# Re-planning a fused attention and mixture-of-experts kernel: a new table of planner constants, and five pieces of work moved or cut finer

## The chip, the cores and the metric

The kernel runs on one core of a Trainium2 chip. The metric is device time in microseconds, the median of several runs. Five engines work side by side, each through its own queue in order: PE (matrix products), ACT (activations), DVE (vector operations), POOL (vector operations and indirect transfers), and SP, which here only issues transfers.

## What is computed

Windowed causal attention over 8 sequences of 576 tokens with 8 heads of 64, then a mixture of 8 experts on its 4608 rows of 512, each row going to its two best experts:

```python
scores = scale * q @ k.T + slope[h] * -|i - j|      # only 0 <= i - j < 128
x = (softmax(scores) @ v) as (4608, 512)
noisy = x @ w_gate + log1p(exp(x @ w_noise)) * noise
top2, weights = two largest of noisy, softmax over the two
out[row] = sum over its two experts e of weight * (relu(x[row] @ w1[e]) @ w2[e])   # 512 -> 1024 -> 512
```

## The kernel before

**A planner writes the program.** The kernel function describes the work as strands (Python generators). Each strand yields operations with an engine, an expected duration and a rank. `Order` (L111) runs them against its own clock: whenever an engine is free it takes the waiting operation of lowest rank (`take`, L171) and writes it into that engine's queue. So the order in all five queues is fixed when the kernel is built, by expected durations and by ranks, which come from the table at L43 to L72. `either` (L280) offers an operation to ACT and, at a rank later by an entry of `LATE`, to DVE; the engine that takes it first has it. On the chip the engines then go through these queues, waiting on semaphores.

**Attention** (32 pairs of heads, four for each sequence). For a pair, PE computes scores (L518), DVE adds the bias and finds the maxima (L524), ACT takes exponentials and their sums into `den` (L532), PE transposes (L539), ACT or DVE copies the result to `pT` (L287 on ACT, L291 on DVE, both helpers that many operations share), and PE multiplies by the values (L553). When a sequence's four pairs are done, `rows` (L659) adds a small constant to `den` in four instructions (L669) and takes the reciprocal (L671); rows of x are transposed, scaled and stored (L701, L704), the gate is computed, and `route` (L782) finds each row's experts and places through a long chain of small steps on DVE, ACT, POOL and PE. An indirect transfer on POOL writes the row numbers into each expert's list.

**Experts.** Products are in float16 with two halves: weights and tokens are scaled by a power of two and split into a high part and the remainder. For a piece of weights (expert e, eighth f; tile `held` or `spare`, 512 KB) that means a maximum (L1143 on DVE, or two activations at L1147 on ACT), the high halves (L287 on ACT or L289 on DVE) and the low halves (L1185 on DVE, or L1182 and L1183 on POOL). Tokens are gathered from memory by POOL (L1218), given a scale (`fit`, L492 to L1235, five small DVE steps), split (`xt`, L287 or L289 and then L1256) and transposed by a transfer that SP issues (L1264) into `ax` or `bx`.

A block of up to 512 tokens then goes through eight pieces. PE computes the first products of a piece (L1273, 12 of them), ACT or DVE writes the rectified high half `ahh` or `bhh` (L1301 or L1303), DVE the low half `ahl` or `bhl` (L1324), and PE the second products (L1333, or L1338 for flipped blocks). Results are scaled by `gw` and added to the output by POOL (L1468).

The first two experts (e < EARLY) are worked on early, in four steps of 256, 256, 256 and 192 tokens each, while attention is still running and just behind it; their eight blocks follow `SEQUENCE`. All other work comes behind attention: the rest of these two experts, then the six late ones in three blocks each.

`overflow` (L1539) makes a table of tokens beyond an expert's capacity, by small vector operations on one partition; a loop at the end (L1651) works through it. In the profiled run no pass of this loop is seen.

Of the kernel before, what the change touches and what calls it, by code (L numbers as in the profile page):

```python
# [41 lines left out]
LISTS = ((0, EARLY, DONE[-1], (CAP - DONE[-1] + 127) // 128), (EARLY, E, 0, (CAP + 127) // 128))  # L42
ZERO = 714.8  # L43
LOAD = 296.4
VALUES = 533.9
GATE = (-2.7, -33.5)
ROUTE = 0
SCATTER = (-245.2, -812.9, 94.5)
FFN0, FFN1 = 207.0, 403.8
WEIGHTS = ((-24.5, 112.1), (505.6, 7.5))  # L50
SEQUENCE = ((0, 0), (0, 1), (1, 0), (1, 1), (0, 2), (1, 2), (0, 3), (1, 3))
TOKENS = -211.8
STAGE = (130.6, -162.3, -306.6, -45.6, -45.9, -85.0, 118.1, -29.9)
MIDDLE = 410.3
RESULT = -460.1
WEIGHTS_LATE = 152.7
SOON = 370.9
LISTED = (-405.9, 168.6)
BIG, PARTS = -57.2, 468.7
TIGHT = (1, 5, 7)  # L60
LATE = (-344.6, -113.3, -185.1, 116.9, -276.1, 92.1, -240.2, -276.5, 251.3, -261.2, 47.5, 142.3, 39.7, 106.3)
LAG = 0.2
SP_COST = 0.55
DMA_RATE = 360e3
DMA_LAG = 4.0
REST = 5.6
PACE = (8.9, 10.6)
HOLD = (-83.6, 40.7)
AHEAD = -25.9
GATHER_LAG, SCATTER_LAG, LISTED_LAG, TURN_LAG = 4.4, 5.0, 3.0, 4.0  # L70
STAY, TURN = -100.0, 0.13
TICK, WARM = 3.413, 1.28  # L72
# [8 lines left out]
class Event:  # L81


    def __init__(self, count=1):
        self.count, self.waiters = count, []


class Op:


    def __init__(self, on, emit, join=True, shape=0, slows=0.0):
        self.slows = slows
        self.on, self.emit, self.join, self.taken = on, emit, join, False
        self.shape, self.leaves = shape if isinstance(shape, tuple) else (shape, shape)
# [16 lines left out]
class Order:  # L111
# [73 lines left out]
    def cost(self, e, us, what):  # L185
        if e == "PE":
            us, self.shape = us + (TURN if what.shape != self.shape else 0.0), what.leaves
        elif e == "POOL" and what.slows:
            self.busy["DVE"] = max(self.busy["DVE"], self.now) + what.slows
            self.at(self.busy["DVE"], lambda: self.dispatch("DVE"))  # L190
        return us
# [56 lines left out]
def attention_moe(ctx: ExitStack, tc: tile.TileContext, qk_, v, w_gate, w_noise, noise, w12,  # L248
# [410 lines left out]
    def rows(b, t):  # L659
# [4 lines left out]

        def turned():
            for e in range(2):
                for h in range(2):
                    from_ = (h + e) % 2 * 64
                    nc.vector.tensor_scalar(den[e * 64:e * 64 + 64, 0:NQ - e, h:H:2], dens[b][from_:from_ + 64, e:NS:2], 1e-9, None,  # L669
                                            op0=OP.add)  # L670
            nc.vector.reciprocal(den, den)  # L671

        yield dve(1.3, rank, turned)
        put(denr, dens[b])
# [107 lines left out]
    def route(b):  # L782
# [347 lines left out]
    def weight(e, f, t, rank):  # L1130
# [44 lines left out]
    def split(e, f, z, t, parts, rank, both):  # L1175
# [208 lines left out]
    def last_downs(blk, rank):  # L1384
# [154 lines left out]
    def overflow():  # L1539
# [19 lines left out]

        def compare():  # L1560
            V.tensor_tensor(ge[:, 0], jt[:, :, None].to_broadcast(shape), cnt[:, 3:4].to_broadcast(shape), op=OP.is_ge)
            V.tensor_mul(ge[:, 1], ge[:, 0], cnt[:, 1:2].to_broadcast(shape))

        def rows():
            V.tensor_reduce(red, ge, axis=AX.X, op=OP.add)
            V.tensor_scalar(red[:, 0], red[:, 0], float(E - 1), None, op0=OP.min)
            V.tensor_sub(red[:, 1], jt, red[:, 1])
            V.tensor_copy(tab[:, 0], red[:, 0])
            V.tensor_tensor(ge[:, 0], iota8[0:1, None, :].to_broadcast(shape), red[:, 0, :, None].to_broadcast(shape), op=OP.is_equal)
            V.tensor_mul(ge[:, 0], ge[:, 0], capv[:, None, :].to_broadcast(shape))  # L1570
            V.tensor_reduce(jt, ge[:, 0], axis=AX.X, op=OP.add)
            V.scalar_tensor_tensor(red[:, 1], red[:, 1], float(128 // UNIT), jt, op0=OP.mult, op1=OP.add)
            V.scalar_tensor_tensor(red[:, 1], red[:, 0], float(EROWS // UNIT), red[:, 1], op0=OP.mult, op1=OP.add)
            V.tensor_scalar(tab[:, 1], red[:, 1], float((E * EROWS - 128) // UNIT), None, op0=OP.min)
# [154 lines left out]
```

## Time and profile before

| | |
|---|---|
| median of 3 runs | 1053.86 us (1053.57 to 1054.55) |
| profiled execution | 1055.3 us, of which the span of the trace is 1053.5 |
| PE busy | 1014.3 us |
| DVE busy | 633.3 us |
| ACT busy | 495.2 us |
| POOL busy | 346.4 us |

A row of a group reads: line, engine, operation, output<-inputs, shape, count, then busy time and the mean duration of one in nanoseconds, then the idle time of the engine in front of them and what ended it. A matmul's own duration (379 ns for 512 columns) is longer than the distance to the next one, since they are pipelined; rates are read from counts over a stretch.

### The profile page before, as it was taken

Reading aid. Unit: us, or ns where it says so; the run is one execution under the profiler, and the core shown is the slowest. Engines: PE = TensorE matmul, PEld = TensorE weight load, DVE = VectorE, ACT = ScalarE, POOL = GpSimd, SP = SyncE. Lnnn points to the kernel's source line nnn. Section 1 sums busy time; section 2 is a strip of 40 time slices with the busy share of each in tenths; the row PEclk is TensorE's granted clock in tenths of the full one; section 3 lists DMA queues with packets and bytes.
Section 4 is the critical chain, followed back from the end, with each engine's and each line's share of the span. In section 5 each row is a group of like instructions: output and inputs, shape, how many; then the busy total and the mean of one; then the engine's idle time right before and its main releaser. Section 6 shows DMA issues by size and latency. Waiting matters only on the chain.

```text
span 1053.5 us, 23716 instructions
## 1 busy us (share of the span) xinstructions
PE 1014.3 (96%) x8942; PEld 639.7 (61%) x8942; DVE 633.3 (60%) x2264; ACT 495.2 (47%) x1402; POOL 346.4 (33%) x458
## 2 busy tenths in 40 slices
PE   7989798999999899999999999999999999999997
PEld 4756666776676579754565457545744664564455
DVE  8998998978787982254559544744494364332111
ACT  8998887766422552231346333632353343332211
POOL 1476963334233431330333232312332320421102
PEclk9999999999999999999999999999999999999999
DMA  9868796635258882385765576519563752653113
GB/s 339 329 233 284 249 305 202 184 96 122 35 108 247 172 105 38 87 190 171 103 144 107 112 151 126 124 40 173 122 135 50 150 82 51 122 68 52 17 24 50
DMA packets 130340, 144.79 MB, mean 137 GB/s; under 512 B 90400, under 2 KB 91504, under 8 KB 130224
## 3 DMA queue, kind: packets, MB, share of 16 engines
q1 hardware_dynamic: 112704, 103.92, 36.1%
q0 software_dynamic: 17520, 39.34, 21.8%
q8 instruction: 71, 1.16, 0.5%
q14 instruction: 45, 0.37, 0.1%
HBM read 82.89 MB, written 40.91 MB: 118 GB/s over the span
## 4 chain that ended last, share of the span: by engine, by line
PE 81%; DVE 12%; ACT 4%; issue 2%; POOL 1%; DMA 0%; DVEq 0%; POOLq 0%; ACTq 0%
PE bank L1273 34%; PE bank L1333 28%; PE bank L1338 6%; PE bank L553 4%; PE bank L518 3%; PE bank L539 3%; DVE p L524 3%; ACT p L532 2%; DVE held L1185 1%; DVE x L704 1%; PE bank L724 1%; ACT pT L287 1%; DVE xt L1256 1%; PE bank L1446 1%; PE bank L701 1%
## 5 line engine op out<-in xcount | busy, mean ns | idle before, releaser
L1273 PEld LDWEIGHTS <-held 128*128 128x128 f16 x2424 | 234.7, 98 | 124.5 <-issue 0.6
L1273 PE MATMUL bank<-bx,held 128*128 128x512 f16 (+7 forms) x1752 | 300.6, 324 | 0.0
L1324 DVE SCALAR_TENSOR_TENSOR bhl<-bank,bhh 128x384 f16<-128x384 f32 (+6 forms) x152 | 84.6, 557 | 281.2 <-ACT bhh L1301 281.0
L1468 POOL DMA_INDIRECT out_dram<-yo,ix x62 | 99.4, 1603 | 426.6 <-ACT yo L287 366.8
L1301 ACT ACTIVATE bhh<-bank 128x512 f16<-128x512 f32 (+6 forms) x134 | 65.4, 488 | 325.9 <-PE bank L1273 317.2
L1333 PE MATMUL bank<-held,bhh 128*128 128x512 f16 x696 | 207.0, 379 | 0.0
L1333 PE MATMUL bank<-held,bhl 128*128 128x512 f16 x348 | 131.9, 379 | 0.0
L532 ACT ACTIVATE p<-p,nm 128x192 f32<-128x192 f32 (+2 forms) x288 | 121.9, 428 | 14.0 <-DVE nm L524 13.6
L1333 PEld LDWEIGHTS <-bhh 128*128 128x128 f16 x768 | 75.2, 98 | 80.7
L1218 POOL DMA_INDIRECT xg<-xs_dram,ix x62 | 69.2, 1116 | 51.9 <-issue 16.6
L524 DVE CUSTOM_DVE_ANT_0 p<-bank,bias 128x192 f32<-128x192 f32 (+2 forms) x288 | 79.6, 328 | 9.5 <-PE bank L518 6.6
L518 PE MATMUL bank<-qk 64*64 64x192 f32 (+2 forms) x1152 | 67.0, 328 | 12.2 <-DVE nm L524 8.5
L1273 PE MATMUL bank<-ax,held 128*128 128x256 f16 (+1 forms) x672 | 77.0, 268 | 0.0
L539 PE MATMUL bank<-ident,p 128*128 128x128 f32 x416 | 67.5, 285 | 9.2 <-ACT pT L287 2.2
L287 ACT ACTIVATE held<-held,wsc 128x512 f16<-128x512 f32 x96 | 65.7, 716 | 17.6 <-DVE held L1185 16.2
L1333 PEld LDWEIGHTS <-bhl 128*128 128x128 f16 x384 | 37.6, 98 | 45.5 <-DVE bhl L1324 0.5
L539 PEld LDWEIGHTS bank<-ident,p 128*128 128x128 f32 x416 | 44.7, 141 | 31.9 <-ACT p L532 10.5
L1143 DVE TENSOR_REDUCE wam<-held 128x2 f32<-128x1024 f32 x53 | 63.7, 1210 | 0.3 <-DMA held<-in_w_dram 0.3
L1185 DVE SCALAR_TENSOR_TENSOR held<-held,wsc,held 128x512 f16<-128x512 f32 x88 | 63.2, 756 | 0.0
L553 PE MATMUL bank<-pT,vraw 64*64 64x64 f32 (+1 forms) x2048 | 61.3, 227 | 0.4 <-DVE x L704 0.3
L553 PEld LDWEIGHTS bank<-pT,vraw 64*64 64x64 f32 (+1 forms) x2048 | 55.1, 138 | 8.8 <-issue 3.5
L287 ACT ACTIVATE xt<-xg,fit 128x512 f16<-128x512 f32 (+5 forms) x60 | 43.0, 718 | 32.6 <-DVE fit L1232 30.9
(254 smaller groups left out, 1499.3 us busy)
## 6 DMA issues: line engine op xcount, KB each, us to landing
held<-in_w_dram SPq DMA_DIRECT2D x60, 512.0 KB
qk<-in_qk_dram SPq DMA_DIRECT2D x31, 576.0 KB
vraw<-in_v_dram SPq DMA_DIRECT2D x16, 640.0 KB
out_dram<-xg SPq DMA_DIRECT2D x10, 1024.0 KB
xs_dram<-x SPq DMA_DIRECT2D x32, 256.0 KB
spare<-in_w_dram SPq DMA_DIRECT2D x4, 512.0 KB
xs_dram<-x SPq DMA_DIRECT2D x8, 128.0 KB
xs_dram<-xg SPq DMA_DIRECT2D x1, 1024.0 KB
```

Of the source, the lines that this page charges most:

```text
L287: nc.scalar.activation(o, i, AF.Copy, **kw)
L518: nc.tensor.matmul(s[j % 2][half:half + 64, o:o + c], qk[rows, j * 64:j * 64 + 64], qk[rows, k1 - c:k1], start=True, stop=True)
L524: nc.vector.tensor_tensor_reduce(out=p[:, place(j):place(j) + c], in0=s[z][:, o:o + c], in1=bias4[:, g, z, 192 - c:192], scale=-0.125, sca ...
L532: nc.scalar.activation(pv, pv, AF.Exp, bias=nm[:, z:z + 1], scale=-1.0, accum_out=den[:, j, g:g + 1])
L539: nc.tensor.transpose(t[:, z * 128:z * 128 + 128], p[:, a * 128:a * 128 + 128], ident)
L553: nc.tensor.matmul(o[half, j // 2 * SUB:j // 2 * SUB + SUB], t[rows, block, hh:hh + D], pt[rows, slot, from_:from_ + 64], start=first_, st ...
L1185: nc.vector.scalar_tensor_tensor(lo, t, sc, hi, op0=OP.mult, op1=OP.subtract)
L1218: yield pool(1.04, rank, lambda: nc.gpsimd.indirect_dma_start(out=xg[0:r], out_offset=None, in_=xs[0:blk.rows], in_offset=bass.IndirectOff ...
L1273: nc.tensor.matmul(t[:, 0:blk.n], wp[:, c], blk.x[:, x + c, 0:blk.n], start=c == 0 and z == 0, stop=c == 3 and z == 2)
L1324: yield dve(0.07 + c * 0.00104, rank - MIDDLE, lambda: nc.vector.scalar_tensor_tensor(hl[:, 0:c], t[:, 0:c], 0.0, hh[:, 0:c], op0=OP.max, ...
L1333: nc.tensor.matmul(blk.y[j][0:r], h[:, cs], wp, start=f == 0 and m == 0, stop=f == 7 and m == 2)
L1468: ins = nc.gpsimd.indirect_dma_start(out=out, out_offset=bass.IndirectOffsetOnAxis(ap=blk.ix[0:r, j:j + 1], axis=0), in_=t[0:r], in_offset ...
```

## The change

The table gets new values throughout (some thirty numbers, `LATE` one more), so that every queue is written in another order. Two lines of it, and then the code:

```diff
-LATE = (-344.6, -113.3, -185.1, 116.9, -276.1, 92.1, -240.2, -276.5, 251.3, -261.2, 47.5, 142.3, 39.7, 106.3)
+LATE = (-420.2, -197.2, -210.3, 89.8, -368.1, 104.7, -72.6, -248.8, -209.9, -164.6, 178.0, 93.5, 45.4, 294.5, 154.1)
-REST = 5.6
+REST = 18.2
...
-        elif e == "POOL" and what.slows:
-            self.busy["DVE"] = max(self.busy["DVE"], self.now) + what.slows
-            self.at(self.busy["DVE"], lambda: self.dispatch("DVE"))
...
-        def turned():
+        on = nc.vector if b == B - 1 else nc.gpsimd
+
+        def collected():
...
-                    nc.vector.tensor_scalar(den[e * 64:e * 64 + 64, 0:NQ - e, h:H:2], dens[b][from_:from_ + 64, e:NS:2], 1e-9, None,
-                                            op0=OP.add)
-            nc.vector.reciprocal(den, den)
-        yield dve(1.3, rank, turned)
+                    on.tensor_scalar(den[e * 64:e * 64 + 64, 0:NQ - e, h:H:2], dens[b][from_:from_ + 64, e:NS:2], 1e-9, None,
+                                     op0=OP.add)
+        yield (dve if b == B - 1 else pool)(1.0, rank, collected)
+        yield dve(0.36, rank, lambda: nc.vector.reciprocal(den, den))
...
-        if e < EARLY:
-            yield either(1.35, 1.13, rank, LATE[12], largest)
-        else:
-            yield dve(1.13, rank + BIG, lambda: largest("DVE"))
+        yield either(1.6, 1.13, rank + (BIG if e >= EARLY else 0), LATE[12 if e < EARLY else 14], largest)
...
-        if e < EARLY:
-            yield Op((("POOL", 2.85, rank), ("DVE", 0.66, rank + WEIGHTS_LATE)), low, slows=0.6)
+        if e <= EARLY:
+            yield Op((("POOL", 2.85, rank), ("DVE", 0.66, rank + WEIGHTS_LATE)), low)
...
-        for z, on in enumerate(("ACT", "DVE")):
+        for z, on in enumerate(("ACT", "ACT")):
...
-        yield dve(1.5, 1110, compare)
-        yield dve(2.2, 1120, rows)
+        for z, (us, emit) in enumerate(steps_):
+            yield dve(us, 1130 + 2 * z, emit)
```

In words: the planner no longer reckons with POOL slowing DVE down (`slows`). The four sums of `den` go to POOL for all sequences but the last. The maxima of late experts' weights may go to ACT too. Low halves of the first late expert (e = 2) may go to POOL. The last half result goes to ACT. And the overflow table, before two operations of two and ten instructions that the planner took for 1.5 and 2.2 us, becomes twelve operations of one instruction (`steps_`, with 6.13 us in all), between which others may be written. REST is the time that the planner keeps between a late weight's expected arrival and its maximum.

Counted over the two orders: 27 of the `pT` copies go from ACT to DVE; 28 of the 32 sums of `den` from DVE to POOL; of the weights' maxima on DVE 57 become 19 and on ACT 7 become 45. PE's operations and SP's are the same in number.

Three places where this moves instructions. First DVE's queue around the overflow table (tile `spared`), some 320 us into the program. Before:

```order
L1324 SCALAR_TENSOR_TENSOR ahl_211<-bank_67,ahh_208 128x256
L1565 TENSOR_REDUCE spared<-spared 1x160
L1566 TENSOR_SCALAR spared<-spared 1x80
L1567 TENSOR_TENSOR spared<-spared 1x80
L1568 CAST bias_135<-spared 1x80
L1569 TENSOR_TENSOR spared<-iota_142,spared 1x640
L1570 TENSOR_TENSOR spared<-spared,capv 1x640
L1571 TENSOR_REDUCE spared<-spared 1x80
L1572 SCALAR_TENSOR_TENSOR spared<-spared 1x80
L1573 SCALAR_TENSOR_TENSOR spared<-spared 1x80
L1574 TENSOR_SCALAR bias_135<-spared 1x80
L1324 SCALAR_TENSOR_TENSOR ahl_212<-bank_71,ahh_209 128x256
```

and after, with the line numbers of the changed kernel (L1319 is the low half, L1556 to L1567 the table):

```order
L1556 TENSOR_TENSOR spared<-spared 1x640
L1557 TENSOR_TENSOR spared<-spared 1x640
L1558 TENSOR_REDUCE spared<-spared 1x160
L1319 SCALAR_TENSOR_TENSOR ahl_213<-bank_67,ahh_210 128x256
...
L1562 TENSOR_TENSOR spared<-iota_142,spared 1x640
L1319 SCALAR_TENSOR_TENSOR ahl_211<-bank_71,ahh_208 128x256
L1563 TENSOR_TENSOR spared<-spared,capv 1x640
L1564 TENSOR_REDUCE spared<-spared 1x80
L1319 SCALAR_TENSOR_TENSOR ahl_212<-bank_66,ahh_209 128x256
L1565 SCALAR_TENSOR_TENSOR spared<-spared 1x80
```

Low halves now stand between the table's steps. Second, DVE's queue where the maxima of the first late expert stood (L1143). Before:

```order
L1324 SCALAR_TENSOR_TENSOR ahl_212<-bank_71,ahh_209 128x256
L1143 TENSOR_REDUCE wam<-held_5068 128x2
L289 TENSOR_SCALAR yo_204<-bank_70,gw_201 128x512
L1143 TENSOR_REDUCE wam<-held_5069 128x2
L1143 TENSOR_REDUCE wam<-held_5070 128x2
L1143 TENSOR_REDUCE wam<-held_5071 128x2
L1143 TENSOR_REDUCE wam<-held_5072 128x2
L1324 SCALAR_TENSOR_TENSOR ahl_213<-bank_66,ahh_210 128x256
```

and after, at the one that is left (L1141), from one low half (L1319) to the next; L1298 is the high half on DVE, L1251 the low part of `xt`, L285 its high part:

```order
L1319 SCALAR_TENSOR_TENSOR ahl_213<-bank_67,ahh_210 128x256
...
L1240 TENSOR_REDUCE fit_215<-xg_5154 128x1
L1141 TENSOR_REDUCE wam<-held_5147 128x2
...
L1251 SCALAR_TENSOR_TENSOR xt_217<-xg_131,fit_214,xt_217 128x512
L1597 TENSOR_SCALAR gw_199<-gw_199,back 128x2
L285 TENSOR_SCALAR xt_218<-xg_5154,fit_215 128x512
L1298 TENSOR_SCALAR ahh_208<-bank_71 128x256
L1251 SCALAR_TENSOR_TENSOR xt_218<-xg_5154,fit_215,xt_218 128x512
L1319 SCALAR_TENSOR_TENSOR ahl_211<-bank_71,ahh_208 128x256
```

Seven of the eight maxima have left for ACT's queue, and a step of the tokens' preparation stands between the high and the low half of one piece; the lines left out are ten small steps of `fit`. Third, PE's queue at the end of the fifth early block, whose last piece is `held_118`, with tokens `ax_206`; the next block has `ax_207`. Before (one row of each run of equal ones):

```order
L1273 MATMUL bank_67<-ax_206,held_118 128x256
...
L1333 MATMUL bank_73<-held_117,ahh_210 128x512
...
L1273 MATMUL bank_71<-ax_207,held_119 128x256
...
L1333 MATMUL bank_73<-held_118,ahh_208 128x512
```

and after (L1268 the first products, L1328 the second):

```order
L1328 MATMUL bank_73<-held_117,ahh_210 128x512
...
L1268 MATMUL bank_71<-ax_206,held_118 128x256
...
L1328 MATMUL bank_69<-held_118,ahh_208 128x512
...
L1268 MATMUL bank_66<-ax_207,held_119 128x256
```

The first products of the last piece are now followed directly by its second products, and the next block's come behind these.

More of the change, by code (lines that the diff above doesn't have):

```diff
@@ L42 @@
 LISTS = ((0, EARLY, DONE[-1], (CAP - DONE[-1] + 127) // 128), (EARLY, E, 0, (CAP + 127) // 128))
[L43 to L46, printed above, removed]
+ZERO = 676.1
+LOAD = 11.7
+VALUES = 513.6
+GATE = (2.6, -95.0)
 ROUTE = 0
-SCATTER = (-245.2, -812.9, 94.5)
-FFN0, FFN1 = 207.0, 403.8
-WEIGHTS = ((-24.5, 112.1), (505.6, 7.5))
+SCATTER = (-173.9, -902.1, 111.7)
+FFN0, FFN1 = 215.6, 417.9
+WEIGHTS = ((-18.9, 110.4), (520.9, 17.2))
 SEQUENCE = ((0, 0), (0, 1), (1, 0), (1, 1), (0, 2), (1, 2), (0, 3), (1, 3))
[L52 to L59, printed above, removed]
+TOKENS = -146.1
+STAGE = (148.4, -265.5, -236.1, -37.2, 42.7, -130.4, 122.5, -310.3)
+MIDDLE = 600.8
+RESULT = -335.5
+WEIGHTS_LATE = 190.3
+SOON = 350.7
+LISTED = (-461.8, 175.9)
+BIG, PARTS = -87.3, 410.2
 TIGHT = (1, 5, 7)
-LATE = (-344.6, -113.3, -185.1, 116.9, -276.1, 92.1, -240.2, -276.5, 251.3, -261.2, 47.5, 142.3, 39.7, 106.3)
+LATE = (-420.2, -197.2, -210.3, 89.8, -368.1, 104.7, -72.6, -248.8, -209.9, -164.6, 178.0, 93.5, 45.4, 294.5, 154.1)
 LAG = 0.2
@@ L65 @@
 DMA_LAG = 4.0
-REST = 5.6
-PACE = (8.9, 10.6)
-HOLD = (-83.6, 40.7)
-AHEAD = -25.9
+REST = 18.2
+PACE = (1.2, 10.6)
+HOLD = (-175.1, 40.7)
+AHEAD = -57.1
 GATHER_LAG, SCATTER_LAG, LISTED_LAG, TURN_LAG = 4.4, 5.0, 3.0, 4.0
-STAY, TURN = -100.0, 0.13
+STAY, TURN = -73.0, 0.13
 TICK, WARM = 3.413, 1.28
@@ L88, with __init__ @@
 class Op:
-    def __init__(self, on, emit, join=True, shape=0, slows=0.0):
-        self.slows = slows
+    def __init__(self, on, emit, join=True, shape=0):
         self.on, self.emit, self.join, self.taken = on, emit, join, False
@@ L943, in route @@
         else:
-            yield Op((("POOL", 1.55, rank), ("DVE", 0.8, rank + LATE[10])), lambda g: tables(engine[g], 2), slows=0.4)
+            yield Op((("POOL", 1.55, rank), ("DVE", 0.8, rank + LATE[10])), lambda g: tables(engine[g], 2))
         a = yield (tb, rank)
@@ L1558, in count @@
             V.tensor_scalar(capv, capv, 1.0 / UNIT, None, op0=OP.mult)
[L1560 to L1574, printed above, removed]
+        steps_ = (
+            (0.75, lambda: V.tensor_tensor(ge[:, 0], jt[:, :, None].to_broadcast(shape), cnt[:, 3:4].to_broadcast(shape), op=OP.is_ge)),
+            (0.75, lambda: V.tensor_mul(ge[:, 1], ge[:, 0], cnt[:, 1:2].to_broadcast(shape))),
+            (1.43, lambda: V.tensor_reduce(red, ge, axis=AX.X, op=OP.add)),
+            (0.12, lambda: V.tensor_scalar(red[:, 0], red[:, 0], float(E - 1), None, op0=OP.min)),
+            (0.15, lambda: V.tensor_sub(red[:, 1], jt, red[:, 1])),
+            (0.1, lambda: V.tensor_copy(tab[:, 0], red[:, 0])),
+            (0.76, lambda: V.tensor_tensor(ge[:, 0], iota8[0:1, None, :].to_broadcast(shape), red[:, 0, :, None].to_broadcast(shape), op=OP.is_equal)),
+            (0.76, lambda: V.tensor_mul(ge[:, 0], ge[:, 0], capv[:, None, :].to_broadcast(shape))),
+            (0.76, lambda: V.tensor_reduce(jt, ge[:, 0], axis=AX.X, op=OP.add)),
+            (0.2, lambda: V.scalar_tensor_tensor(red[:, 1], red[:, 1], float(128 // UNIT), jt, op0=OP.mult, op1=OP.add)),
+            (0.2, lambda: V.scalar_tensor_tensor(red[:, 1], red[:, 0], float(EROWS // UNIT), red[:, 1], op0=OP.mult, op1=OP.add)),
+            (0.15, lambda: V.tensor_scalar(tab[:, 1], red[:, 1], float((E * EROWS - 128) // UNIT), None, op0=OP.min)),
+        )
```

## Prediction

> **What bounds the kernel now.** I read the page first (busy shares, chain), then busy time by stage, then PE's waits in the stage that lost most, then the timeline around the two longest of them. The page's busy share and chain:
>
> ```profile
> PE 1014.3 (96%) x8942; PEld 639.7 (61%) x8942; DVE 633.3 (60%) x2264; ACT 495.2 (47%) x1402; POOL 346.4 (33%) x458
> PE 81%; DVE 12%; ACT 4%; issue 2%; POOL 1%; DMA 0%; DVEq 0%; POOLq 0%; ACTq 0%
> ```
>
> PE is the bound, but not evenly. Busy time in stretches (columns: PE, PEld, DVE, ACT, POOL, granted clock, DMA share, GB/s):
>
> ```profile
> 0.00:200.00 200.00, 175.73 (x3078) 127.89 (x3079) 178.57 (x836) 171.26 (x657) 106.14 (x159) 0.98 0.80 271
> 200.00:320.00 120.00, 118.20 (x1462) 85.72 (x1463) 93.86 (x442) 58.85 (x213) 44.55 (x85) 1.00 0.42 99
> 320.00:390.00 70.00, 64.74 (x423) 40.95 (x421) 61.95 (x188) 33.41 (x71) 22.75 (x26) 0.98 0.89 184
> 390.00:1045.00 655.00, 655.00 (x3981) 384.70 (x3979) 298.41 (x799) 231.66 (x463) 171.45 (x188) 1.00 0.52 100
> ```
>
> and four of the slices of 25 us, same columns:
>
> ```profile
> 325.00:350.00 25.00, 20.90 (x130) 12.78 (x128) 22.31 (x52) 7.26 (x19) 7.39 (x9) 0.94 0.92 245
> 350.00:375.00 25.00, 23.95 (x159) 15.07 (x158) 22.47 (x83) 16.26 (x33) 10.53 (x12) 0.99 0.80 165
> ...
> 475.00:500.00 25.00, 25.00 (x117) 11.34 (x116) 10.31 (x16) 4.15 (x7) 2.23 (x3) 1.00 0.55 175
> ...
> 550.00:575.00 25.00, 25.00 (x162) 15.74 (x160) 24.00 (x56) 17.41 (x32) 4.81 (x5) 1.00 0.55 109
> ```
>
> Three kinds of stage. In the first 200 us (attention alone) PE idles 24.3 us while DVE is 89% and ACT 86% busy. From 390 to 1045 us PE never idles and runs at rate: 117 products in 25 us, 214 ns for 512 columns. The same products are issued before and after the change, so these 655 us can only grow. Between them, 320 to 390 us loses 5.26 us idle, and the clock loses 6% and 1% of two 25 us slices, 1.75 us: 7.0 us that an order could save. PE's waits from 300 to 400 us name DVE (total, times, longest; the one other wait, 2.2 us, is in the timeline below):
>
> ```profile
> PE bank L1333 <- DVE ahl L1324: 2.8, 3, 1.9
> ```
>
> **The table and the maxima (320 to 350 us).** First the overflow table, in the timeline:
>
> ```profile
> 327.26 1.46 DVE L1565 TENSOR_REDUCE spared<-spared 1x160 f32<-1x1280 f32 x1
> ...
> 329.98 0.81 DVE L1570 TENSOR_TENSOR spared<-spared,capv 1x640 f32<-1x640 f32 x1
> ...
> 332.32 0.40 DVE L1324 SCALAR_TENSOR_TENSOR ahl<-bank,ahh 128x256 f16<-128x256 f32 x1
> ...
> 332.78 0.39 PE L1333 MATMUL bank<-held,ahl 128*128 128x512 f16 x1 [1.90 <-DVE ahl L1324]
> ```
>
> The ten instructions of `rows` hold DVE for 5.06 us (327.26 to 332.32), and the low half that PE needs is queued behind all ten. After the change they are twelve separate steps with low halves between them. The longest run without one is nine small steps and the three of 0.81, 0.81 and 1.46, and there the PE order has two more first products (held_124, held_126) and a second product before it needs the result, some 4 us. I count the 1.90 us as gone.
>
> Then the maxima of the first late expert:
>
> ```profile
> 340.71 2.78 PE L1273 MATMUL bank<-ax,spare 128*128 128x256 f16 x24
> 341.44 4.59 DVE L1143 TENSOR_REDUCE wam<-held 128x2 f32<-128x1024 f32 x4
> 343.62 0.61 PE L1333 MATMUL bank<-spare,ahh 128*128 128x512 f16 x2
> 346.28 0.15 DVE L492 TENSOR_SCALAR fit<-fit 128x1 int32<-128x1 int32 x1
> 346.42 0.39 PE L1333 MATMUL bank<-spare,ahl 128*128 128x512 f16 x1 [2.20 <-DVE fit L492]
> ```
>
> Four maxima in a row (4.59 us) hold up a low half; PE idles 2.20 us, and the clock's 0.94 falls into this slice. After, seven of these eight maxima are on ACT: 2 x (629 + 193) = 1.64 us each, and five high halves of that time (some 0.4 us each) go to DVE.
>
> ```profile
> L1147 ACT ACTIVATE junk<-held 128x512 bf16<-128x512 f32 x14 | 8.8, 629 | 0.2
> L1147 ACT ACTIVATION_READ_ACCUMULATOR junk<-held 128x1 f32 x14 | 2.7, 193 | 0.0
> ```
>
> Cover: ACT is 33.41 of 70 us busy, so 7 x 1.64 = 11.5 us fit. The 2.20 us and the 1.75 us of clock go.
>
> What is late next stands in the PE order: at the end of the fifth block the first products of the last piece (held_118) are followed at once by its second products; the next block's come only behind them. Before, that block's first products stood in between. The new gap is priced by DVE's queue there. Durations, from the view of one line (min/median/max) and from groups of instructions:
>
> ```profile
> L1245 DVE TENSOR_REDUCE fit<-xg x7: 674/675/680, 232.3 to 638.6; 128x1 f32<-128x512 f32 x7
> ```
> ```profile
> L1143 DVE TENSOR_REDUCE wam<-held 128x2 f32<-128x1024 f32 x53 | 63.7, 1210 | 0.3 <-DMA held<-in_w_dram 0.3
> ```
> ```profile
> L1324 DVE SCALAR_TENSOR_TENSOR ahl<-bank,ahh 128x256 f16<-128x256 f32 x18 | 7.3, 411 | 2.5 <-ACT ahh L1301 2.5
> ...
> L1256 DVE SCALAR_TENSOR_TENSOR xt<-xg,fit,xt 128x512 f16<-128x512 f32 x6 | 4.4, 742 | 0.0
> ...
> L289 DVE TENSOR_SCALAR xt<-xg,fit 128x512 f16<-128x512 f32 x3 | 1.4, 479 | 0.0
> ```
>
> From the previous low half to this piece's high half (both on DVE now) stand 11 steps of 0.15, one of 0.675, the one maximum left (1.21), 0.742 and 0.479: 4.8 us. PE has six products of 214 ns and twelve of half that, 2.6 us. So the high half starts 2.2 us late, takes about 0.4 (as L1324), and the low half comes 0.742 + 0.411 behind it while PE has two products, 0.43 us: 0.7 more. That makes 1.1 us where DVE has no backlog and 3.3 where it has all of it. I take 2.4, nearer the backlog, as DVE is over 22 of 25 us busy there. Half speed may follow such a gap, as it did the 2.20: half of 1.75 is 0.9. The remaining small waits on L1324 (2.8 - 1.9 = 0.9 us) stay. Stage: -1.90 - 2.20 - 1.75 + 2.4 + 0.9 = **-2.5 us**, between -0.8 (3.3 and the whole 1.75) and -4.8 (1.1 and full speed).
>
> **Attention (0 to 300 us).**
>
> ```profile
> L291 DVE COPY pT<-bank 128x384 f32<-128x384 f32 x31 | 16.5, 542 | 0.4 <-PE bank L539 0.4
> ...
> L291 DVE COPY pT<-bank 128x256 f32<-128x256 f32 x19 | 7.9, 415 | 1.1 <-PE bank L539 1.1
> L1185 DVE SCALAR_TENSOR_TENSOR held<-held,wsc,held 128x512 f16<-128x512 f32 x8 | 7.5, 936 | 0.0
> ...
> L669 DVE TENSOR_SCALAR byrow<-den 64x16 f32<-64x16 f32 x16 | 5.1, 320 | 0.2
> ...
> L669 DVE TENSOR_SCALAR byrow<-den 64x20 f32<-64x20 f32 x16 | 2.6, 164 | 0.1
> ```
>
> and from the groups of ACT and POOL and the view of L1185 over the whole span:
>
> ```profile
> L287 ACT ACTIVATE pT<-bank 128x384 f32<-128x384 f32 x65 | 30.6, 487 | 11.0 <-PE bank L539 8.0 <-DVE nm L524 1.5 <-DVE idx L802 1.1
> L287 ACT ACTIVATE pT<-bank 128x256 f32<-128x256 f32 x45 | 16.4, 375 | 8.1 <-PE bank L539 6.9 <-DVE tp L798 1.2
> ```
> ```profile
> L1182 POOL TENSOR_SCALAR held<-held,wsc 128x512 f32<-128x512 f32 x24 | 39.4, 1640 | 42.2 <-DVE spare L289 36.8 <-ACT held L287 5.3
> L1183 POOL TENSOR_TENSOR held<-held,held 128x512 f16<-128x512 f32 x20 | 23.3, 1165 | 1.7
> ...
> L888 POOL TENSOR_SCALAR d<-d 128x5 f32<-128x5 f32 x7 | 1.8, 253 | 4.2 <-ACT d L927 3.9
> ```
> ```profile
> L1185 DVE SCALAR_TENSOR_TENSOR held<-held,wsc,held x88: 728/739/1383, 49.9 to 878.2; 128x512 f16<-128x512 f32 x88
> ```
>
> Counted in the two orders: 27 of the transposed-score copies go from ACT to DVE (12 of 542 ns, 15 of 415): +12.7 us for DVE, -11.5 for ACT. The 28 sums of `den` leave DVE: -(14 x 0.320 + 14 x 0.164) = -6.8. Five low halves of early weights move from POOL to DVE inside attention (5 x 0.74 to 0.94, some +4): net **+10 us on DVE, -11 on ACT**; POOL loses 5 x 2.8 = 14 us and gains 28 x about 0.25 = 7. DVE idles 21 us of the first 200, so part of the 10 is covered, and the rest comes onto the path, a loss of 0 to 10. Against that, PE's first FFN product comes one pair of heads earlier in its order (25 pairs in, not 26), so one pair's work (200 us / 26 = 7.7 us) runs where PE idles 1.5% (200 to 320) and not 12%: -0.8. And POOL, 106 of 200 us busy, is 7 us lighter: the routing that the first FFN block waits for passes POOL after the weights' low halves, two of them (5.6 us) standing between two of its steps. DVE too is held up less: the 64x16 sums average 320 ns beside 164 for the larger 64x20, and early low halves 936 beside a median of 739: 16 x 0.16 + 8 x 0.2 = 4 us lost to something. I take +1.5 of the 10 as uncovered, -0.8, and -2 for POOL, under a third of the 7: **-1.3 us**, from +8 (little is covered) to -4.
>
> What could hold DVE there: the Trainium skill, page "SBUF — State Buffer", section "Who interferes with whom", says that a DVE instruction with two SBUF inputs and a GpSimd instruction that reads SBUF exclude each other, the second one to start blocking fully. The 320 beside 164 ns agrees with that. By this rule 28 sums on POOL and the dropped allowance `slows` speak against the change; the rival below has it.
>
> **The rest at nothing.** Late maxima on ACT (from 400 us): 1.64 for 1.21 us; even where DVE is 24.00 of 25 us busy (550 to 575) PE stays at 25.00, and each piece has 1.3 us or more of other products between its first and second ones there, as before. Were that cover gone, each maximum in front of a high half would cost up to 1.64. REST grows by 12.6, so that ACT doesn't stand before a weight still in flight. The last half result goes from DVE to ACT, 0.48 us against 0.47:
>
> ```profile
> 1043.05 0.47 ACT L287 ACTIVATE yo<-bank,gw 112x256 f32<-112x256 f32 x1 [1.88 <-PE bank L1414]
> ...
> 1045.67 0.48 DVE L289 TENSOR_SCALAR yo<-bank,gw 112x256 f32<-112x256 f32 x1 [9.61 <-PE bank L1414]
> ```
>
> Sum: -2.5 - 1.3 = **-3.8 us**. The profiled execution took 1055.3 us (span 1053.5), 1.4 above the median of 1053.86: I expect a profiled 1051.5 and a median of **1050.1 us**.
>
> **Rivals.** (A) Slower: DVE becomes attention's bound. Price: 8 of its 10 us uncovered, POOL no help, the stage at 320 us as forecast: +8 - 0.8 - 2.5 = +4.7, **1058.6**. For it: 89% busy already, POOL's sums holding it up. Against: 21 us idle. It breaks even at 3.3 us uncovered and is measurably slower from 5.4. (B) No change: what is saved comes back at the new gap (3.3 + 1.75 against 5.85) with attention at 0: -0.8, **1053.1**. For it: the backlog of 4.8 us. Against: the clock must halve fully too. (C) A large gain: POOL's relief brings the routing forward by as much as a pair's 7.7 us and DVE gets its 4 us back, of which I count 4 in all, and the gap is the small one: -4 - 4.8 = -8.8, **1045.1**. For it: POOL is 53% busy in attention and DVE loses time beside it. Against: DVE's +10.
>
> **How the numbers follow.** Forecast 0.42, A 0.24, B 0.17, C 0.17. 0.2% is 2.1 us, about what a measurement can tell from no change: faster is below 1051.75, slower above 1055.97. The forecast's own spread puts 0.36 of its 0.42 below that bound and 0.06 in the band; C is faster, B the same, and 0.03 of A falls into the band. Faster 0.36 + 0.17 = 0.53, same 0.06 + 0.17 + 0.03 = 0.26, slower 0.21. Range: down to C with a microsecond for its unknowns, 1044; up to just short of A, 1058, so that about one in ten is left out on each side. The forecast's own range is 1047 to 1053.
>
> **What would show it.** Right: in the changed profile no PE wait over 1 us on the table, one PE wait of 1 to 3 us behind the last piece of the fifth block, PE 100% busy from 390 us on, PE idle of 22 to 24 us in the first 200 us. Wrong: DVE over 92% busy there and PE idle 28 or more (A); PE idle 20 or less, with the first FFN product 4 us or more earlier (C); any PE idle after 400 us breaks the term at nothing.

## The result and the profile after

The changed kernel takes **1067.19 us** (median of 4 runs, 1065.19 to 1068.50), the kernel before beside it 1054.20: ratio 1.0111, 95% interval 1.0095 to 1.0127. It is 13 us slower. The forecast was 1050.1, with a range up to 1058.

Busy shares from the page of the changed kernel, then its time by the same four stages and by four slices of 25 us (columns as before):

```profile
PE 1017.5 (95%) x8942; PEld 642.5 (60%) x8942; DVE 613.8 (58%) x2256; ACT 519.4 (49%) x1491; POOL 367.7 (34%) x487
```
```profile
0.00:200.00 200.00, 168.63 (x2930) 123.65 (x2930) 174.96 (x810) 158.13 (x609) 101.12 (x168) 0.97 0.79 265
200.00:320.00 120.00, 117.67 (x1534) 84.66 (x1529) 90.97 (x429) 62.83 (x235) 44.10 (x90) 1.00 0.46 109
320.00:390.00 70.00, 68.81 (x486) 45.83 (x483) 55.33 (x193) 33.32 (x84) 32.00 (x31) 1.00 0.70 168
390.00:1045.00 655.00, 649.32 (x3907) 378.38 (x3908) 291.28 (x824) 262.37 (x560) 187.26 (x194) 0.99 0.53 101
```
```profile
150.00:175.00 25.00, 18.36 (x365) 13.48 (x368) 15.40 (x93) 15.08 (x65) 7.02 (x21) 0.97 0.78 263
175.00:200.00 25.00, 22.11 (x373) 16.96 (x365) 22.77 (x120) 19.47 (x79) 8.16 (x16) 0.90 0.62 169
325.00:350.00 25.00, 25.00 (x185) 17.30 (x184) 19.33 (x60) 7.16 (x17) 8.60 (x11) 1.00 0.72 195
375.00:400.00 25.00, 19.89 (x118) 11.47 (x116) 24.27 (x74) 13.18 (x29) 19.95 (x15) 0.90 0.59 127
```

Three of these slices in the kernel before, for comparison:

```profile
150.00:175.00 25.00, 23.86 (x453) 17.90 (x449) 20.77 (x113) 16.68 (x70) 9.87 (x23) 1.00 0.77 251
175.00:200.00 25.00, 22.04 (x402) 15.74 (x401) 24.11 (x130) 21.70 (x89) 5.95 (x15) 1.00 0.69 185
375.00:400.00 25.00, 24.89 (x225) 19.74 (x223) 18.32 (x56) 11.39 (x25) 5.57 (x7) 1.00 0.85 102
```

Three things are to be seen. PE idles 31.4 of the first 200 us (24.3 before), although DVE is *less* busy there than before (174.96 against 178.57): something stands still, nothing is overloaded. The slice from 325 to 350 us, which lost 4.1 us idle and 6% of the clock before, now loses nothing. And a new hole opens from 375 to 400 us: 5.1 us idle and, in this run, 10% of the clock. Two rows of PE's waits say the same (total, times, longest), and the first of them before:

```profile
PE bank L514 <- DVE nm L520: 13.6, 17, 5.1
PE bank L1328 <- DVE ahl L1319: 5.0, 3, 3.2
```
```profile
PE bank L518 <- DVE nm L524: 8.5, 14, 1.6
```

**The hole at 169 us.** PE's wait of 5.1 us is for DVE's maxima, and DVE stands too. Timelines of POOL, of DVE and of PE:

```profile
163.15 1.02 POOL L1213 DMA_INDIRECT xg<-xs_dram,cl  x1 [3.68 <-DVE ef L875]
...
164.79 1.00 POOL L1213 DMA_INDIRECT xg<-xs_dram,cl  x1 [0.16 <-issue]
165.85 0.29 POOL L667 TENSOR_SCALAR byrow<-den 64x20 f32<-64x20 f32 x1
171.75 0.90 POOL L667 TENSOR_SCALAR byrow<-den 64x20 f32<-64x20 f32 x3 [5.61 <-DMA xg<-xs_dram,cl]
```
```profile
166.38 0.15 DVE L884 TENSOR_TENSOR base<-base,bank 128x8 f32<-128x8 f32 x1
172.68 0.40 DVE L671 RECIPROCAL byrow<-byrow 128x40 f32<-128x40 f32 x1 [6.16 <-POOL byrow L667]
```
```profile
174.43 1.54 PE L514 MATMUL bank<-qk 64*64 64x192 f32 x12 [5.09 <-DVE nm L520]
```

POOL issues two gathers of tokens, does the first of the four `den` sums, and then waits 5.61 us before the second, until the second gather has landed. The sums have nothing to do with the gathered tokens. But the program makes them wait, as the changed kernel's list for POOL shows with its semaphores (DMASW are POOL's own transfers):

```
L1213 DMA xg1_132<-xs_dram,cl0_184 128x520
L667 TENSOR_SCALAR byrow1_104<-den1_101 64x20
L667 TENSOR_SCALAR byrow1_104<-den1_101 64x20 [waits DMASW2_49,DMASW3_49,DMASW1_49,Pool_49]
L667 TENSOR_SCALAR byrow1_104<-den1_101 64x16 x2
```

The second sum, the first of the four that reads from partition 64 on, waits for three earlier transfers of POOL; in four of the seven sequences there are such to wait for. On DVE, before, the same sums carried no such wait; why the program gives it to them on POOL is not known. Behind it stands DVE's reciprocal, behind that all of DVE's attention work, behind that ACT and PE. I had read the order without its waits.

**The hole at 390 us.** The rows that matter of PE, DVE and POOL:

```profile
394.10 0.39 PE L1328 MATMUL bank<-held,ahl 128*128 128x512 f16 x1 [3.17 <-DVE ahl L1319]
...
397.24 0.61 PE L1328 MATMUL bank<-held,ahl 128*128 128x512 f16 x1 [1.41 <-DVE ahl L1319]
```
```profile
387.28 2.31 DVE L1180 SCALAR_TENSOR_TENSOR held<-held,wsc,held 128x512 f16<-128x512 f32 x2
...
391.42 1.63 DVE L1180 SCALAR_TENSOR_TENSOR held<-held,wsc,held 128x512 f16<-128x512 f32 x1
392.97 0.74 DVE L1251 SCALAR_TENSOR_TENSOR xt<-xg,fit,xt 128x512 f16<-128x512 f32 x1
393.63 0.41 DVE L1319 SCALAR_TENSOR_TENSOR ahl<-bank,ahh 128x256 f16<-128x256 f32 x1
393.97 1.28 DVE L1180 SCALAR_TENSOR_TENSOR held<-held,wsc,held 128x512 f16<-128x512 f32 x1
...
395.78 1.06 DVE L1233 SCALAR_TENSOR_TENSOR xg<-xg,fit,chosen 128x8 f32<-128x8 f32 x1
396.77 0.41 DVE L1319 SCALAR_TENSOR_TENSOR ahl<-bank,ahh 128x256 f16<-128x256 f32 x1
```
```profile
389.02 2.20 POOL L1177 TENSOR_SCALAR held<-held,wsc 128x512 f32<-128x512 f32 x1
391.30 1.20 POOL L1178 TENSOR_TENSOR held<-held,held 128x512 f16<-128x512 f32 x1
...
394.00 1.58 POOL L1177 TENSOR_SCALAR held<-held,wsc 128x512 f32<-128x512 f32 x1
395.67 1.15 POOL L1178 TENSOR_TENSOR held<-held,held 128x512 f16<-128x512 f32 x1
```

The low halves of activations that PE needs (L1319) stand behind low halves of weights (L1180), which take 1.28 and 1.63 us here and 0.74 elsewhere; one step of the token weights (L1233) takes 1.06 instead of 0.23. Beside them POOL works on low halves of the same expert, the first late one, which the change allowed it (`e <= EARLY`).

### The profile page after: what moved, and what is told of

It reads as the page before. It is cut to its first block, busy times and chain, and to the rows that moved or that the text cites. A ratio compares the mean times of both kernels' runs of the same rounds, so it can differ in the third digit from the quotient of the medians.

```text
span 1065.9 us, 23848 instructions
## 1 busy us (share of the span) xinstructions
PE 1017.5 (95%) x8942; PEld 642.5 (60%) x8942; DVE 613.8 (58%) x2256; ACT 519.4 (49%) x1491; POOL 367.7 (34%) x487
## 3 DMA queue, kind: packets, MB, share of 16 engines
q8 instruction: 71, 1.16, 0.5%
## 4 chain that ended last, share of the span: by engine, by line
PE 82%; DVE 13%; issue 2%; ACT 1%; POOL 1%; DMA 1%; SPq 0%; DVEq 0%; POOLq 0%; ACTq 0%
PE bank L1268 35%; PE bank L1328 28%; PE bank L1333 6%; PE bank L549 4%; DVE p L520 3%; PE bank L514 3%; PE bank L535 3%; DVE pT L287 1%; DVE held L1180 1%; DVE x L702 1%; PE bank L699 1%; PE bank L1441 1%; ACT p L528 1%; DMA xg<-xs_dram,cl 1%; DVE xt L1251 1%
## 5 line engine op out<-in xcount | busy, mean ns | idle before, releaser
L1268 PEld LDWEIGHTS <-held 128*128 128x128 f16 x2424 | 234.2, 98 | 124.0 <-issue 1.2
L1268 PE MATMUL bank<-bx,held 128*128 128x512 f16 (+7 forms) x1752 | 301.7, 324 | 0.0
L1319 DVE SCALAR_TENSOR_TENSOR bhl<-bank,bhh 128x384 f16<-128x384 f32 (+6 forms) x152 | 84.6, 557 | 282.7 <-ACT bhh L1296 280.8
L1328 PE MATMUL bank<-held,bhh 128*128 128x512 f16 x696 | 207.0, 379 | 0.0
L1296 ACT ACTIVATE bhh<-bank 128x384 f16<-128x384 f32 (+6 forms) x122 | 59.5, 488 | 298.1 <-PE bank L1268 289.8
L1328 PE MATMUL bank<-held,bhl 128*128 128x512 f16 x348 | 131.9, 379 | 0.0
L1328 PEld LDWEIGHTS <-bhh 128*128 128x128 f16 x768 | 75.0, 98 | 80.6
L1213 POOL DMA_INDIRECT xg<-xs_dram,ix x62 | 76.5, 1234 | 29.1 <-issue 14.0
L1268 PE MATMUL bank<-ax,held 128*128 128x256 f16 (+1 forms) x672 | 75.0, 266 | 0.6 <-DVE ahl L1319 0.5
L283 ACT ACTIVATE held<-held,wsc 128x512 f16<-128x512 f32 x93 | 62.7, 714 | 14.7 <-DVE held L1180 8.3
L1180 DVE SCALAR_TENSOR_TENSOR held<-held,wsc,held 128x512 f16<-128x512 f32 x86 | 66.0, 808 | 0.0
L1328 PEld LDWEIGHTS <-bhl 128*128 128x128 f16 x384 | 37.6, 98 | 45.3
L514 PEld LDWEIGHTS bank<-qk 64*64 64x64 f32 x1152 | 42.1, 140 | 31.9 <-DVE nm L520 21.1
L1251 DVE SCALAR_TENSOR_TENSOR xt<-xg,fit,xt 128x512 f16<-128x512 f32 x78 | 57.5, 745 | 1.3 <-ACT xt L283 1.1
```

Source lines behind the costliest of these rows:

```text
L514: nc.tensor.matmul(s[j % 2][half:half + 64, o:o + c], qk[rows, j * 64:j * 64 + 64], qk[rows, k1 - c:k1], start=True, stop=True)
L1180: nc.vector.scalar_tensor_tensor(lo, t, sc, hi, op0=OP.mult, op1=OP.subtract)
L1213: yield pool(1.04, rank, lambda: nc.gpsimd.indirect_dma_start(out=xg[0:r], out_offset=None, in_=xs[0:blk.rows], in_offset=bass.IndirectOff ...
L1251: yield dve(0.66, rank, lambda: V.scalar_tensor_tensor(lo, xg[0:r, 0:DM], up_, hi, op0=OP.mult, op1=OP.subtract))
L1268: nc.tensor.matmul(t[:, 0:blk.n], wp[:, c], blk.x[:, x + c, 0:blk.n], start=c == 0 and z == 0, stop=c == 3 and z == 2)
L1319: yield dve(0.07 + c * 0.00104, rank - MIDDLE, lambda: nc.vector.scalar_tensor_tensor(hl[:, 0:c], t[:, 0:c], 0.0, hh[:, 0:c], op0=OP.max, ...
```

## The experiments

Theory **W**: the sums' wait for POOL's transfers makes attention slower. Theory **L**: POOL's low halves near 390 us make that hole. Rivals: **D**, DVE carries too much in attention, or **C**, it does so by the 27 more copies (not the prediction's rival C); **O**, it is the new order as such. The runs come in four groups, each on one chip, and only kernels of one group are compared closely: the kernel before took 1052.22, 1055.38, 1055.38 and 1054.49 us in them. "Loss" in the expectations is a stretch's time less a fixed time for each product that PE starts in it, by its shape; only its differences between kernels count. Up to 325 us and from 325 to 425 us it is 58.9 and 9.4 us before, 68.8 and 11.9 in the changed kernel. "Order kept" means that the planner's decisions are the same and only the engine that an operation is written to differs. All these kernels compute everything.

**Sums and low halves, order kept.** half_sums:

```diff
+                if from_ in froms:
...
-        yield (dve if b == B - 1 else pool)(1.0, rank, collected)
-        yield dve(0.36, rank, lambda: nc.vector.reciprocal(den, den))
+        yield (dve if b == B - 1 else pool)(1.0, rank, lambda: collected(on, (0,)))
+        yield dve(0.36, rank, lambda: (collected(nc.vector, (64,)), nc.vector.reciprocal(den, den)))
```

> The changed kernel with every engine's order kept; only the two of each four den sums that read from partition 64 on go from POOL to DVE, just ahead of their reciprocal (14 sums of 160 to 320 ns, about 3 us more on DVE). Theory W: in the changed kernel the second sum at 165.9 us stands 5.6 us until POOL's own gathers have landed, DVE's reciprocal behind it 6.2 us and PE 5.1 us, and PE runs at half speed after it; the wait belongs to the sums that read from partition 64 on. Then the 5.1 us and 1 to 2 us of clock go: 1060 to 1062.5 us, and no DVE wait over 1 us on POOL byrow. Rival D: attention is slow because DVE carries more work; then 3 us more on DVE give nothing or cost up to 3: 1066 to 1070.

all_sums has `()` and `(0, 64)` for `(0,)` and `(64,)`:

> The changed kernel with every engine's order kept; all four den sums of a batch go from POOL to DVE, just ahead of their reciprocal (28 sums, about 6 us more on DVE, as before the change). Theory W: the same gain as with half of them, 5 to 7 us, less at most 1 to 2 for the other 3 us of DVE work: 1060 to 1064 us. Rival D: DVE's work decides, so this one is slower than the changed kernel by 2 to 6: 1069 to 1073.

low_dve:

```diff
-            yield Op((("POOL", 2.85, rank), ("DVE", 0.66, rank + WEIGHTS_LATE)), low)
+            yield Op((("POOL", 2.85, rank), ("DVE", 0.66, rank + WEIGHTS_LATE)), low if e < EARLY else lambda g: low("DVE"))
```

> The changed kernel with every engine's order kept; the five low halves of the first late expert that it put on POOL (380 to 400 us, 2.8 to 3.7 us each) are emitted on DVE in the same places (0.74 us each). Theory L: the 5.7 us that PE loses from 389 to 398 us come from DVE's low halves taking 1.28 to 1.63 us each instead of 0.74 and the maximum's step 1.06 instead of 0.23 while POOL works on the same kind; without POOL there they take 0.74, and 3 to 5 of the 5.7 us go, with some clock: 1062 to 1064.5 us. Rival O: the loss is that of the order (first and second products of one piece back to back) and DVE has 3.7 us more to do there: 1066.5 to 1070.

half_and_low has both edits:

> The changed kernel with both edits (half of the den sums and the five low halves on DVE), order kept. W and L together: the two places are 220 us apart and add up, 1056 to 1059 us, still 2 to 5 above the kernel before, because attention's order as such is no better. If one of them only shifts the loss to the other, the sum is smaller than the two gains by 2 us or more.

Measured on one chip: half_sums 1061.27 us (1.0082, interval 1.0069 to 1.0095), all_sums 1061.04 (1.0081), low_dve 1064.42 (1.0112), half_and_low 1058.86 (1.0066). The second edit takes 2.4 us off half_sums, and the first 5.6 off low_dve. That 14 more sums on DVE (3 us) change nothing, all_sums against half_sums, speaks against D. The changed kernel did not run on this chip, and low_dve's ratio is that of the changed kernel elsewhere (1.0111 to 1.0118): by itself its edit is not shown to gain. In its profile PE is busy for 22.85 of the 25 us from 375 to 400 us (19.89 in the changed kernel), but DVE's wait for the sums, 7.7 us, is longer than in any run of the changed kernel. For the sizes of single edits the runs were repeated beside the changed kernel on another chip:

> The changed kernel unaltered, for the three others of this call: ratio 1.010 to 1.0125 as twice before.

> Half of the den sums on DVE again, now on the same chip as the changed kernel. Theory W: 5 to 7 us below the changed kernel of this call (by the two profiles' losses up to 325 us, 68.8 against 63.7). If the ratios of the two calls hold (1.0115 and 1.0082): 3 to 4 us.

> Both edits again. Theory L: 2 to 3.5 us below half_sums_2 (by the profiles, 11.0 against 8.2 us lost from 325 to 425); if POOL's low halves cost nothing on the path, within 1 us of it.

Measured: changed_third **1066.70**, half_sums_2 **1060.80**, half_and_low_2 **1057.78** us (ratios 1.0118, 1.0059 and 1.0032, the last 1.0020 to 1.0043). So W is worth **5.9 us** and L, with half of the sums back on DVE, **3.0 us**, both as expected; the intervals leave 1 to 2 us of doubt on each. Ratios do not carry from chip to chip: half_sums went from 1.0082 to 1.0059, half_and_low from 1.0066 to 1.0032. In half_sums_2, PE's row for the same wait and DVE's for the sums, then the slice that held the hole:

```profile
PE bank L514 <- DVE nm L520: 7.8, 15, 1.3
```
```profile
DVE byrow L671 <- POOL byrow L667: 0.3, 1, 0.3
```
```profile
150.00:175.00 25.00, 22.94 (x402) 16.46 (x400) 21.95 (x125) 21.32 (x89) 7.61 (x20) 1.00 0.88 285
```

In half_and_low_2, the second hole's slice (POOL 7.39 us busy, not 19.95, and the clock full) and what is left of the wait, then one of DVE's low halves, of which the others up to 395 us take 0.70 to 0.74 each too:

```profile
375.00:400.00 25.00, 21.80 (x192) 16.62 (x190) 23.88 (x71) 15.24 (x33) 7.39 (x8) 1.00 0.64 134
```
```profile
387.19 0.39 PE L1328 MATMUL bank<-held,ahl 128*128 128x512 f16 x1 [1.69 <-DVE ahl L1319]
```
```profile
385.39 0.74 DVE L1180 SCALAR_TENSOR_TENSOR held<-held,wsc,held 128x512 f16<-128x512 f32 x1
```

DVE has five low halves more to do in this run and is still sooner. The trace agrees with the rule that the prediction took from the Trainium skill (page "SBUF — State Buffer", section "Who interferes with whom"): a DVE step with two SBUF inputs is held up by a POOL step that reads SBUF. Not each overlap costs DVE time, though: in the changed kernel L1251 at 386.61 us and L1233 at 390.12 us took their usual 0.74 and 0.23 us inside a POOL step L1177, and those two POOL steps took 2.00 and 2.20 us, for a median of 1.57.

**The sums on POOL in the old order.** old_sums_on_pool, the kernel before, order kept:

```diff
-                    nc.vector.tensor_scalar(den[e * 64
+                    (nc.vector if b == B - 1 else nc.gpsimd).tensor_scalar(den[e * 64
```

> The kernel before with every engine's order kept; the 28 den sums of all batches but the last are emitted on POOL instead of DVE at the same places, about 6 us less on DVE. Theory W: the sums that read from partition 64 on wait for POOL's own DMAs (in this order scatters and gathers stand ahead of four of the seven batches) and all sums stand behind POOL's low halves, so DVE's reciprocals wait several times for 1 to 6 us: slower by 5 to 12 us. Rival D: DVE is relieved by 6 us where it is 89% busy: faster by 2 to 4 us.

Measured 1059.30 us, ratio 1.0040 (1.0025 to 1.0054): slower by some 4 us, a little less than expected, though DVE has less work. D falls. Its DVE waits, then POOL's rows ahead of the longest of them (2.29 us, until 140.45) and at the one place where POOL stood before a second sum:

```profile
DVE byrow L671 <- POOL byrow L669: 7.5, 6, 2.3
```
```profile
137.95 1.16 POOL L1183 TENSOR_TENSOR held<-held,held 128x512 f16<-128x512 f32 x1
139.21 1.21 POOL L669 TENSOR_SCALAR byrow<-den 64x20 f32<-64x20 f32 x4
```
```profile
245.93 1.32 POOL L669 TENSOR_SCALAR byrow<-den 64x20 f32<-64x20 f32 x3 [1.53 <-issue]
```

Here it is mostly not the landing of a transfer that DVE waits for, though four of the seven sequences carry such waits in this order too. Only at 245.93 us did POOL stand for one, 1.53 us, of which 0.39 reached DVE. In the other five the four sums ran without a gap and were late because they stood in POOL's queue behind low halves of weights or routing steps. So this run shows the price of the sums' place in POOL's queue; W as seen at 169 us is shown in the changed kernel's order alone.

A control, the changed kernel:

> The changed kernel unaltered, on the same chip as the three others of this call, to have its ratio beside theirs: slower by 1.0 to 1.3%, as at first, with the DVE wait of 5 to 6 us on POOL byrow and the PE loss of 5 to 6 us near 390 us again.

Measured 1068.04 us, 1.0115 (1.0098 to 1.0132); the sums' wait was 7.2 us this time and 4.7 in changed_third. Each time this wait ended with the landing of a gather.

**The table and the maxima, each alone in the kernel before.** They are `steps_` in place of `compare` and `rows`, and

```diff
-            yield dve(1.13, rank + BIG, lambda: largest("DVE"))
+            yield either(1.6, 1.13, rank + BIG, 154.1, largest)
```

The planner then gives a new order from about 300 us on; attention stays as it was.

> The kernel before with two parts of the change alone: the overflow table in twelve steps, and the late experts' maxima on ACT or DVE (bias 154.1); sums on DVE, low halves of the first late expert on DVE, all numbers of the table old, attention's order as before. Theory L (the gap near 390 us in the changed kernel is made by POOL's low halves): the 7.0 us lost from 320 to 350 us go and a small gap comes, 2.5 to 5 us faster than the kernel before. Rival O (the gap is the order's): a gap as large as the saving comes without POOL's low halves too, and the time stays within 1 us of the kernel before.

> The kernel before with the overflow table in twelve steps and nothing else. The wait of 1.9 us behind the table goes; with the maxima still on DVE their wait of 2.2 us stays: 1 to 2.5 us faster than the kernel before (ratio 0.9977 to 0.999). If what DVE leaves undone is only taken up later, no change (0.9995 to 1.0005).

> The kernel before with the late experts' maxima on ACT or DVE (bias 154.1) and nothing else. By my forecast the 2.2 us and part of 1.75 us of clock go, and a gap behind the last piece comes in their place: 0 to 3 us faster (0.997 to 1.0). By the run with both parts (no change): the gap takes back what is saved, within 1 us (0.999 to 1.001).

Measured 1054.93 (1.0000, interval 0.9990 to 1.0009), 1055.64 (0.9998, 0.9990 to 1.0007) and 1054.92 us (0.9994, 0.9985 to 1.0002): **no gain** that the measurement can tell, alone or together. The wait that each was to remove is gone, and another of the same size stands some microseconds later. One row of PE's waits of each, in the order both, table, maxima:

```profile
PE bank L1333 <- DVE ahh L1303: 2.3, 2, 2.2
```
```profile
PE bank L1273 <- issue: 2.1, 1, 2.1
```
```profile
PE bank L484 <- DVE ix L1008: 1.8, 1, 1.8
```

With the table alone PE is ready for the next block's first products at about 338.9 us, 1.8 before the 340.7 of the kernel before, but stands 2.1 us and starts them at 341.0. The row names no releaser; in the trace this instruction waits on the semaphores of the block's two transposes, which SP had issued from 331.5 us on:

```profile
331.53 5.98 SPq L1264 DMA_TRANSPOSE ax<-xt  x2
```

With the maxima alone, the transposition that the weights' scale needs (L484) is what comes late. With both, PE waits for a high half, before which DVE itself is idle; what DVE waits for there the profile does not show, and that stays open.

**Numbers and code apart.** old_code_new_numbers is the kernel before with the new table of constants, new_code_old_numbers the reverse:

> The kernel before under the changed kernel's numbers (ranks, biases, leads): sums on DVE, table in two steps, late maxima and last half result on DVE. What is left of attention's loss once the sums are off POOL (4 us by the profiles) is either of the new numbers, which put 27 copies on DVE: then attention here loses 3 to 5 us more up to 325 us than in the kernel before, and the whole is slower by 3 to 6; or it is of the new code's order: then attention here is within 1.5 us of the kernel before.

> The changed kernel's code under the old numbers (the one bias that is new is 154.1, as in the changed kernel), planned anew: sums on POOL, table in steps, first late expert's low halves on POOL, maxima on ACT or DVE. If the code's two mechanisms (sums that wait for POOL's gathers, low halves that block DVE) work in any order: 5 to 12 us slower than the kernel before, with DVE waits on POOL byrow of several us in total. If they hang on the new numbers' order: within 3 us of the kernel before.

Measured 1069.87 (1.0132, 1.0113 to 1.0152) and 1070.66 us (1.0141, 1.0126 to 1.0155). Either half alone is as slow as the two together: the parts of such a change do not add up, and each replans all queues. In the second, DVE waits for the sums only 1.6 us, so what W costs hangs on the order, and this run does not confirm W and L as its causes.

**The copies, order kept.** copies_back is half_and_low with

```diff
+    def third(e, seen_=[]): seen_.append(e == "DVE"); return "ACT" if seen_[-1] and sum(seen_) % 3 == 0 else e
...
-        yield either(..., r4, LATE[3], lambda e: evac(e, i, a, pt))
+        yield either(..., r4, LATE[3], lambda e: evac(third(e), i, a, pt))
```

> The kernel of the run half_and_low (ratio 1.0066) with one more edit, order kept: every third of the copies of transposed scores that the changed kernel puts on DVE in attention (25 of 77, 415 or 545 ns each) is emitted on ACT in the same place, so DVE has 12 us less there and about its old number of copies. Theory C: the 4 to 5 us that attention still loses beside the kernel before come from the copies on DVE; then 3 to 5 us go, ratio 1.002 to 1.004. Rival O: they are in the new order of the work, whatever engine copies; then -0.5 to +2 us, ratio 1.006 to 1.009.

Measured 1058.66 us, ratio 1.0029 (1.0018 to 1.0039), which looked like C; but the median was that of half_and_low, and the kernel before was 3 us slower on this chip. On one chip:

> Both edits and every third copy on ACT again. Theory C (the copies on DVE): 3 to 5 us below half_and_low_2, as the two ratios said (1.0066 and 1.0029). Rival O (the order itself): within 1 us of it, as the two medians (1058.86 and 1058.66) and the profiles' losses up to 325 us (63.9 and 63.9) said.

Measured 1057.10 us (1.0028, 1.0019 to 1.0037) beside 1057.78 (1.0032): 0.7 us, and the intervals overlap. **C falls.** DVE is 7 us less busy in attention, ACT 8 us more (231.71 us, as the 232.93 before), and the time stays, as the rows for 0 to 325 us of half_and_low_2 and copies_back_2 show:

```profile
0.00:325.00 325.00, 295.26 (x4541) 215.45 (x4542) 275.47 (x1289) 223.81 (x850) 141.60 (x246) 0.99 0.66 203
```
```profile
0.00:325.00 325.00, 295.45 (x4552) 215.33 (x4553) 268.17 (x1273) 231.71 (x878) 142.98 (x249) 0.99 0.66 204
```

No version beat the kernel before by more than the measurement can tell.

## Why the prediction was wrong

On the last chip the 12.2 us of the changed kernel (1066.70 less 1054.49) are 5.9 of W, 3.0 of L and 3.3 that remain with both edits.

- **The failed step is "-2 for POOL" in the attention term.** I counted the sums moved to POOL as 28 times 0.25 us of work on an engine with room, and looked at what stands ahead of POOL's routing steps. What counts of a moved step is also what it waits for in its new queue, and who waits for it: a sum with a wait for POOL's gathers, and a DVE reciprocal behind it with all of attention behind that. The term was -1.3 with a worst case of +8; attention lost about 10 us more than before (68.8 against 58.9), and 5.9 of the whole were this.
- **DVE's +10 us, "+1.5 uncovered": the load did not rise as counted, and rival A was wrong in its mechanism.** all_sums has every sum on DVE and still only 277.80 us of DVE work up to 325 us, for 276.54 before. The copies are there (24.7 to 37.6 us), but six copies of `xu` and two of `gt` left DVE (16.7 to 14.2 and 4.1 to 2.7 us), which I had not counted, and many steps became a little shorter. A's price (1058.6) was the nearest of the rivals and still 8.6 us short; of its signs PE's idle time came (31.4 us), but not DVE over 92% busy (174.96 of 200 us). DVE was not the bound: all_sums and copies_back_2 move its load by +3 and -7 us without effect. Nor do the 320 beside 164 ns fit the rule on two inputs, as I wrote: the sums read one tensor, `den`. Four of them took 0.41 to 1.16 us, each beside a POOL step.
- **The first FFN product one pair earlier, "-0.8": undone by W.** It starts at 201.5 us in the changed kernel, at 200.3 before and at 195.2 in all_sums, where nothing waits for POOL.
- **Table, maxima and clock, -5.85: they went as forecast** (25.00 of 25 us busy from 325 to 350, clock 1.00). **The gap behind `held_118`, +2.4 and +0.9, was too dear**: PE waits 0.59 us for the high half and 0.39 for the low half there, with no loss of clock. What I missed is the end of the *next* block (`held_126` and `held_125`), where first and second products also stand back to back and POOL's low halves slow DVE's: 0.39 + 3.17 + 1.41 us idle and, in this run, 10% of 25 us of clock, 7.5 us in all, of which the edit for L brings back 3.0. I had stopped at the first place where first and second products stand back to back, and had taken DVE's steps at their medians although I had quoted 936 beside 739 ns for L1185 where POOL is busy.
- **Even the -2.5 of that stage was not to be had by itself**: in the old order the parts bring 0.5 us at most by the medians (1.6 by the intervals), and PE, 2 us sooner, meets the next thing that is late. I had asked what is late next at one place only.
- **The rest at nothing: nearly right.** From 425 us on PE is busy without a gap as before; one wait of 0.8 us on ACT near 417 us is new.
- **Open**: the last 3.3 us (6.6 on the first chip, 1058.86 less 1052.22). By the loss they lie in attention (about 4 to 5 us more than before, less some 1 us won behind it), and neither DVE's copies nor its sums explain them. That leaves the new order as such, which no run took apart further, so O is neither shown nor excluded.

## What to carry to other kernels

Before a step is moved to another queue, read its waits in the new program, not only its duration: a short step on an engine that also issues transfers can be made to wait for their landing, and an in-order consumer passes the wait on to everyone. Where a wait is removed, name the next three things that come due at that place; here each removal of about 2 us met a wait of about the same size within 15 us. And compare single edits with the planner's order held fixed and on one chip: parts that replan everything did not add up, and one ratio from another chip suggested a cause that was none.

## What the runs showed of the hardware

- POOL's gather of 128 rows keeps POOL for about 1.0 us, but DVE, which waited for its landing by way of POOL's sum, stood 6.2, 7.2 and 4.7 us in three runs of one kernel; the DMA engines were 78% busy in the first.
- On DVE beside POOL a low half took up to 1.63 us for 0.74, and the small two-input step L1233 1.06 for 0.23; POOL's own step slowed too, 2.20 us for a median of 1.57.
- The granted clock did not follow the holes closely. With the whole hole at 390 us it was 0.90, 0.89 and 1.00 from 375 to 400 us in three runs of the changed kernel; with POOL's low halves gone, 0.93 in half_and_low and 1.00 in half_and_low_2. After the hole at 169 us it was 0.90 from 175 to 200 us, without it 0.93 in half_sums_2, and 1.00 in the kernel before. So no part of the clock's loss is shown to be the price of either hole.
